# TensorE's instructions untied: placed by their emission order, and free to pass one another

## The chip, the cores and the metric

The kernel runs on one core of a Trainium2 chip. The core has a matrix engine (TensorE, PE in the profile, with PEld for the loading of its weights), VectorE (DVE), ScalarE (ACT), GpSimd (POOL), and SyncE (SP), whose queue issues most of the DMA transfers. Each engine takes its own instructions strictly in the order in which they stand in its queue; between engines, semaphores say when a result is there. Matmuls and transposes write to PSUM, which is cut into banks of 2 KB for each of 128 partitions; the other engines read the banks and so free them.

The metric is the device time of one execution in microseconds; less is better.

## What is computed

Two attentions follow one another. The first has 8 batches of 8 heads, 576 positions and 64 channels a head. Scores below the row's maximum less `tau` are dropped:

```python
scores = scale * np.matmul(q, k.transpose(0, 1, 3, 2))
thresh = np.max(scores, axis=-1, keepdims=True) - tau
scores = np.where(scores >= thresh, scores, -1000000000.0)
attn = softmax(scores)
attn_out = np.matmul(attn, v)
```

Its output, with the heads side by side as x of 576 rows by 512 columns for each batch, goes into a mixture of 4 attention experts of which each row takes its best two:

```python
logits = x @ w_gate                      # 4 a row; the two highest are kept
w = softmax(logits of the two)
for e in range(4):
    q, k, v = x @ wq[e], x @ wk[e], x @ wv[e]          # 64 channels
    a = softmax(causal(scale * (q @ k.T)))
    ye = a @ v @ wo[e]                                  # 512 columns
    out += (w of e, or 0 where e is not among the two) * ye
```

## The kernel before

**Units of work.** The first attention runs over 32 pairs of heads (n = 0 to 31, four to a batch). Each pair has five row tiles: four of 128 rows for each of the two heads, and one, called tile 4, that holds the last 64 rows of both. The main loop (from line 740) goes through 32 x 5 steps; step i takes tile s of pair n in the order `TS = (4, 0, 1, 2, 3)`. The second attention of a batch starts when its four pairs are done, and is spread over the steps of the next batch's pairs.

**The first attention.** `prep` (line 243) scales q and k (qi, ki), transposes them on TensorE (qkT; qkTt for the last 64 rows), splits each into a rounded part and its rest (hl), copies the small pieces (qd) and then spreads hl over partitions with DMAs on SP's queue: eight for the keys (kt), four for the queries (qt). `scores` (line 313) makes a score tile s in PSUM; VectorE finds its maximum (nmx, line 336) and the threshold (thr, line 338), ScalarE the exponential (line 341), VectorE drops what is under the threshold and sums (line 343), and POOL divides (line 351); the result is pp. `transp` (line 361) transposes pp on TensorE (tm, and tt for the last 64 columns) into a PSUM bank, from which ScalarE or VectorE copies it (pt, ptt; line 144 is the copy whose engine the scheduler picks). `attnv` (line 394) multiplies it with v (av) and splits the result into x's rounded part and rest ("xh", "xl", line 426).

**The second attention.** `project` (line 432) makes q2 and k2 of a pair of experts (bank pj); `values` (line 468) makes v2 and the logits, and at its end the gate weights gw. `scores2` (line 527) makes a score tile (s2 in the emitted names, s in the profile's), its maximum (nm) and exponential (p2, line 562). `scale2` (line 566) multiplies p2 on POOL by the gate and the inverse of its sum (line 576): it can run only when the last values of the batch, and the gate after them, are done. `transp2` (line 578) transposes p2 (t2, t2t), `attnv2` (line 601) multiplies it with v2, and `output` (line 626) makes o with wo.

**PSUM.** Score tiles of the first attention, and tile 4 of the second, take one of two double banks (`ps_s`). Everything else that TensorE writes takes one of four banks (`ps_g`) in rotation: the fifth such tile needs what was in the first to be read.

**What sets the order.** The program emits instructions; a scheduler then builds each engine's queue from their dependencies and priorities. `pr(what)` (line 103) sets the priority of what is emitted next: the step, plus an offset in steps from the table `PR`, plus a running number, so that a smaller value comes sooner. TensorE is the exception: `queued` (line 151) ties each matmul and transpose to the one emitted before it, so its queue is the emitted order whatever the table says.

```python
    def pr(what):
        now[1] += 20
        tc.cur_priority = 20000000 + int((now[0] + PR.get(what, 0.0)) * 1000000) + now[1]
```

The emitted order is worked out by a plan. `pe[1]` adds up a modelled time of TensorE in ns. Each step emits its own work and then `fill`s with pieces of the second attention up to the step's `goal`: outputs and transposes that are due, tile-4 scores, and otherwise one more group of projections or values (`project_some`, line 657). A piece is due some modelled ns after what it needs: `AFTER_S2` from a score tile to its transposes, `AFTER_T2` from there to its product, and `AFTER_V = 4500` from a batch's last values to the first transposes that need the gate (line 671). At most three probability tiles p2 are open (`P2B`).

Of the kernel before, what the change touches and what calls it, by code (L numbers as in the profile page):

```python
# [9 lines left out]
F32 = mybir.dt.float32  # L10
# [18 lines left out]
AFTER_S2, AFTER_V, AFTER_T2, AFTER_AV2 = 7000, 4500, 1800, 2000  # L29
BETWEEN_S2 = 2000  # L30
# [4 lines left out]
E_QD = "P"  # L35
# [13 lines left out]
    "s": 0.767, "max": -0.509, "thr": -0.091, "exp": 0.327, "stt": -2.461, "sum": -1.419, "nrm": 0.098,  # L49
# [4 lines left out]
}  # L54
PPB = 4
# [4 lines left out]
E_PT = "XX"  # L60
# [4 lines left out]
def kernel(  # L65
# [177 lines left out]
    def prep(n):  # L243
# [34 lines left out]
        def spread(dst, src):  # L278
            pr("dm")
            nc.sync.dma_start(dst.bitcast(F32), src.bitcast(F32))  # L280
# [10 lines left out]
        copy(E_QD, hl[:, :, KO + S:], hl[:, :, KO:KO + ST].bitcast(F32))  # L291
        for j, sl in enumerate(heads):
            pr("qd")
            copy(E_QD, qd[sl, :, j * ST:(j + 1) * ST], hl[sl, :, SM:KO].bitcast(F32))
        for x in range(2):
            for j, sl in enumerate(heads):

                o = KO if j else KO + ST
                for rows in heads:
                    spread(kt[rows, j, x], hl[sl, x, o:o + S])  # L300
# [60 lines left out]
    def transp(n, s):  # L361
# [4 lines left out]
        for j in range(2 if s < R else 1):  # L366
# [7 lines left out]
            copy(E_PT[j], pt, g)  # L374
# [203 lines left out]
    def transp2(b, t, ep):  # L578
        p2 = P2[b, t, ep][0]
        nch = min(t + 1, R)  # L580
        pts = []
        for j in range(2 if t < R else 1):
            g = gbank(f"t2_{b}_{t}_{ep}_{j}")
            pr("t2")
            for c in range(nch):
                transpose(g[:, c * P:(c + 1) * P], p2[:, j * SM + c * P:j * SM + (c + 1) * P])
            pr("pt2")
            pt = one.tile([P, SM], F32, tag="pt", name=f"pt2_{b}_{t}_{ep}_{j}", bufs=PTB)
            copy(E_PT2, pt[:, :nch * P], g[:, :nch * P])
            pts.append(pt)  # L590
# [237 lines left out]
```

## Time and profile before

| | us |
|---|---|
| runs | 1059.22, 1061.42, 1070.57 |
| median | 1061.42 |
| the profiled execution | 1066.01 |
| its span in the profile | 1064.3 |
| TensorE's mean granted clock in it | 0.984 of full speed |

The page's rows are groups of instructions: line, engine, operation, output<-inputs, how many; then busy time, mean ns of one, and the idle time of that engine just before them with what ended it. These are the groups of the main loop that do not stand in the prediction:

```profile
L351 POOL TENSOR_SCALAR pp<-pp,ss 128x576 f32<-128x576 f32 x288 | 212.4, 748 | 409.7 <-DVE ss L357 310.0
L343 DVE SCALAR_TENSOR_TENSOR pp<-s,thr,pp 128x576 f32<-128x576 f32 x288 | 234.2, 815 | 67.6 <-ACT pp L341 60.0
L341 ACT ACTIVATE pp<-s,nmx 128x576 f32<-128x576 f32 x288 | 214.9, 746 | 113.6 <-DVE nmx L336 112.0
L336 DVE TENSOR_REDUCE nmx<-s 128x1 f32<-128x576 f32 x288 | 215.8, 751 | 32.1 <-PE s L162 31.5
L162 PE MATMUL s<-kt,qt 128*128 128x288 f32 x1024 | 195.4, 314 | 25.6 <-DVE pp L343 10.7
```

A score tile costs VectorE 751 and 815 ns, ScalarE 746 and POOL 748. In the timeline a row has its start, its duration, and in brackets the engine's idle time ahead of it with what ended it. In the table of windows a row has the stretch, its length, the busy time of PE, PEld, DVE, ACT and POOL with their instructions, the granted clock, the DMA share and GB/s. Times count from the start of the span.

### The profile page before, as it was taken

To read this page: it belongs to the slowest core of one execution; us is meant where nothing else is said; L and a number is where in the kernel's file an instruction comes from. 1 tells how busy PE (TensorE), PEld (TensorE's weight loads), DVE (VectorE), ACT (ScalarE), POOL (GpSimd) and SP (SyncE) were. 2 spreads that over 40 slices of the span, in tenths; PEclk is the share of its full clock that TensorE was granted. 3 is DMA by queue.
4 is the path that set the end of the run, shared out by engine and by line. 5 is a ranking of instruction groups with operands and counts; after the bars stand their busy time and mean duration, and the time that the engine had idled before them with its cause. 6 is when DMAs were issued, how large, how long until landed. Compare 5 with 4: busy or idle time off the path is not lost.

```text
span 1064.3 us, 26639 instructions
## 1 busy us (share of the span) xinstructions
PE 966.1 (91%) x9520; PEld 860.6 (81%) x9520; DVE 833.5 (78%) x2411; ACT 636.6 (60%) x1556; POOL 407.8 (38%) x703
## 2 busy tenths in 40 slices
PE   3778979899899998999988999899989999899987
PEld 2777978789888898788887898778978789878875
DVE  3898886887878887888878888878787888778463
ACT  3676656665656665665656656666565756566553
POOL 2565433443434324353244433434343433433122
PEclk9999999999999999999999999999999999999998
DMA  6565421344322433324234442234432243320101
GB/s 164 140 162 143 118 78 33 97 125 108 99 68 56 122 98 99 99 72 116 68 87 99 110 121 70 53 87 124 120 98 58 55 132 99 76 55 13 46 2 45
DMA packets 83890, 96.11 MB, mean 90 GB/s; under 512 B 29744, under 2 KB 54320, under 8 KB 83760
## 3 DMA queue, kind: packets, MB, share of 16 engines
q1 hardware_dynamic: 83760, 94.42, 34.2%
q8 instruction: 76, 1.25, 0.5%
q14 instruction: 54, 0.44, 0.1%
HBM read 30.42 MB, written 9.44 MB: 37 GB/s over the span
## 4 chain that ended last, share of the span: by engine, by line
PE 60%; DVE 16%; ACT 11%; POOL 3%; issue 3%; DMA 0%; DVEq 0%; POOLq 0%; ACTq 0%
PE av L162 18%; PE s L162 13%; PE pj L162 8%; PE o L162 6%; PE tm L165 6%; DVE pp L343 5%; PE v L162 4%; PE t L165 3%; ACT p L562 3%; DVE x L426 2%; ACT pp L341 2%; ACT x L140 2%; POOL p L576 2%; DVE nmx L336 2%; ACT pt L144 2%
## 5 line engine op out<-in xcount | busy, mean ns | idle before, releaser
L351 POOL TENSOR_SCALAR pp<-pp,ss 128x576 f32<-128x576 f32 x288 | 212.4, 748 | 409.7 <-DVE ss L357 310.0
L343 DVE SCALAR_TENSOR_TENSOR pp<-s,thr,pp 128x576 f32<-128x576 f32 x288 | 234.2, 815 | 67.6 <-ACT pp L341 60.0
L341 ACT ACTIVATE pp<-s,nmx 128x576 f32<-128x576 f32 x288 | 214.9, 746 | 113.6 <-DVE nmx L336 112.0
L336 DVE TENSOR_REDUCE nmx<-s 128x1 f32<-128x576 f32 x288 | 215.8, 751 | 32.1 <-PE s L162 31.5
L162 PE MATMUL s<-kt,qt 128*128 128x288 f32 x1024 | 195.4, 314 | 25.6 <-DVE pp L343 10.7
L162 PEld LDWEIGHTS s<-kt,qt 128*128 128x128 f32 x1024 | 151.6, 194 | 38.0 <-issue 16.2
L165 PE MATMUL tm<-ident,pp 128*128 128x128 f32 x1152 | 162.4, 277 | 2.4 <-POOL pp L351 1.8
L162 PE MATMUL av<-pt,vm 128*64 128x128 f32 (+1 forms) x2560 | 157.2, 265 | 0.3
L144 ACT COPY pt<-tm 128x512 f32<-128x512 f32 x195 | 113.0, 588 | 61.7 <-PE tm L165 59.0
L165 PEld LDWEIGHTS tm<-ident,pp 128*128 128x128 f32 x1152 | 138.2, 143 | 4.2 <-POOL pp L351 3.7
L162 PEld LDWEIGHTS av<-pt,vm 128*64 128x64 f32 x2560 | 131.6, 137 | 11.9 <-issue 6.8
L562 ACT ACTIVATE p<-s,nm 128x384 f32<-128x384 f32 (+3 forms) x144 | 78.4, 549 | 66.5 <-DVE nm L560 64.5
L576 POOL TENSOR_SCALAR p<-p,sm,gw 128x512 f32<-128x512 f32 (+3 forms) x128 | 76.6, 606 | 82.6 <-ACT pt L144 33.9
L165 PE MATMUL t<-ident,p 128*128 128x128 f32 x384 | 65.0, 293 | 28.1 <-POOL p L576 21.3
L140 ACT ACTIVATE x<-av 128x256 fp32r<-128x256 f32 (+1 forms) x96 | 48.3, 503 | 70.4 <-PE av L162 49.0
L165 PEld LDWEIGHTS t<-ident,p 128*128 128x128 f32 x384 | 45.1, 147 | 41.5 <-POOL p L576 25.0
L560 DVE TENSOR_REDUCE nm<-s 128x1 f32<-128x384 f32 (+3 forms) x144 | 69.4, 512 | 9.4 <-PE s L162 5.9
L140 ACT ACTIVATE pt<-t 128x512 f32<-128x512 f32 (+2 forms) x144 | 58.7, 457 | 25.3 <-PE t L165 25.0
L144 DVE COPY pt<-tm 128x512 f32<-128x512 f32 x93 | 63.4, 684 | 6.6 <-PE tm L165 6.6
L162 PE MATMUL v<-wvh,x 128*128 128x260 f32 x320 | 67.0, 292 | 1.2 <-ACT p L562 0.3
L426 DVE TENSOR_TENSOR x<-av,x 128x256 fp32r<-128x256 f32 (+1 forms) x96 | 47.5, 494 | 23.1 <-ACT x L140 22.7
L162 PE MATMUL av<-ptt,vtz 128*64 128x128 f32 (+1 forms) x640 | 60.1, 263 | 0.0
(129 smaller groups left out, 1789.2 us busy)
## 6 DMA issues: line engine op xcount, KB each, us to landing
kt<-hl SPq DMA_DIRECT2D x256, 144.0 KB, 2.7
qt<-hl SPq DMA_DIRECT2D x128, 128.0 KB, 2.3
km<-in_k_dram SPq DMA_DIRECT2D x32, 256.0 KB, 2.9
qm<-in_q_dram SPq DMA_DIRECT2D x32, 256.0 KB, 3.0
vm<-in_v_dram SPq DMA_DIRECT2D x32, 256.0 KB, 2.8
out_dram<-ob SPq DMA_DIRECT2D x32, 256.0 KB, 2.4
km<-in_k_dram SPq DMA_DIRECT2D x32, 32.0 KB, 2.5
qm<-in_q_dram SPq DMA_DIRECT2D x32, 32.0 KB, 2.7
```

The source lines that it names most:

```text
L140: nc.scalar.activation(dst, src, AF.Copy)
L144: nc.any.tensor_copy(dst, src)
L162: queued(nc.tensor.matmul(out, x, y, **kw), x, ns if x.shape[0] == P else ns / 2)
L165: queued(nc.tensor.transpose(out, x, ident), x, 109)
L336: nc.vector.tensor_reduce(nmx[:, js], sv, axis=AX.XY, op=ALU.max, negate=True)
L341: nc.scalar.activation(e, sv, AF.Exp, bias=nmx[:, js])
L343: nc.vector.scalar_tensor_tensor(e, sv, thr[:, js], e, op0=ALU.is_ge, op1=ALU.mult, accum_out=ss[:, js])
L351: nc.gpsimd.tensor_scalar(p, p, ss[:, h:h + 1], 0.0, op0=ALU.mult, op1=ALU.add)
L426: nc.vector.tensor_tensor(xl, gs, xh.bitcast(F32), op=ALU.subtract)
L560: nc.vector.tensor_reduce(nmx[:, j:j + 1], sv, axis=AX.X if t < R else AX.XY, op=ALU.max, negate=True)
L562: nc.scalar.activation(p2[:, j * SM:j * SM + w] if t < R else halves(p2[:, :S]), sv, AF.Exp, bias=nmx[:, j:j + 1], accum_out=sm[:, j:j + 1])
L576: nc.gpsimd.tensor_scalar(p, p, sm[:, j:j + 1], gg[:, j:j + 1], op0=ALU.mult, op1=ALU.mult)
```

## The change

TensorE's instructions lose the tie: `queued` keeps only the modelled time. Their priority is the step and the running number alone (`TENSOR`, offset 0), so that the scheduler puts them in emitted order where they are ready in its own simulation, and otherwise lets a ready one pass. The table keeps the other engines' offsets, but that of "xl" goes from 0.858 to -0.15.

With it go changes of the plan and of the first pairs:

- `AFTER_V` is 8500 (5000 after the main loop, `AFTER_V_END`), and steps 0 and 2 call `project_some` once more, ahead of their own transposes. In step 2 `prep` goes on after the first `fill` and no longer before it. Tile 4 of the second attention's scores is emitted at a step's end and not by `piece`; `tiled` loses its argument.
- The loads of pairs 1 and 2 stand in SP's queue behind the last spread of pair 0 (`SPREAD[0]`). For pair 0, the key spreads of its second head go to ScalarE's queue (behind `SPREAD[1]`, the last split), qd is copied by VectorE, and tau is loaded first, on ScalarE's queue.
- Copies of tm out of PSUM go to ScalarE for pairs 0 to 3; from pair 4 on the scheduler picks ScalarE or VectorE as before (`E_PT` goes).
- `transp2` puts both experts' transposes in one bank with one copy where they fit (tiles 0 and 1).

```diff
-AFTER_S2, AFTER_V, AFTER_T2, AFTER_AV2 = 7000, 4500, 1800, 2000
-BETWEEN_S2 = 2000
+AFTER_S2, AFTER_V, AFTER_T2, AFTER_AV2 = 7000, 8500, 1800, 2000
+BETWEEN_S2, AFTER_V_END = 2000, 5000
...
-    "av": -4, "xh": -0.154, "xl": 0.858, "pj": 1.006, "q2": -0.353, "v2": 0.393, "v2e": 0.385,
+    "xh": -0.154, "xl": -0.15, "q2": -0.353, "v2e": 0.385,
...
+TENSOR = ("s", "qkT", "tm", "tt", "av", "pj", "v2", "s2", "t2", "av2", "o")
-E_PT = "XX"
...
-        tc.cur_priority = 20000000 + int((now[0] + PR.get(what, 0.0)) * 1000000) + now[1]
+        tc.cur_priority = 20000000 + int((now[0] + (0.0 if what in TENSOR else PR[what])) * 1000000) + now[1]
...
     def queued(r, x, ns):
-        if pe[0] is not None:
-            tc.add_manual_dep(r.ins, pe[0].name,
-                              mybir.DependencyInfo(mybir.DependencyClass.NoSync, mybir.DependencyReason.DATA),
-                              reason="order")
...
+        def load(dst, src):
+            r = nc.sync.dma_start(dst, src)
+            if n in (1, 2):
+                tc.add_manual_dep(r.ins, SPREAD[0].name, NOSYNC, reason="order")
...
-        def spread(dst, src):
+        def spread(dst, src, e=nc.sync):
             pr("dm")
-            nc.sync.dma_start(dst.bitcast(F32), src.bitcast(F32))
+            r = e.dma_start(dst.bitcast(F32), src.bitcast(F32))
+            if n == 0 and e is nc.sync:
+                SPREAD[0] = r.ins
+            elif n == 0:
+                tc.add_manual_dep(r.ins, SPREAD[1].name, NOSYNC, reason="order")
...
-        copy(E_QD, hl[:, :, KO + S:], hl[:, :, KO:KO + ST].bitcast(F32))
+        e = "D" if n == 0 else E_QD
+        copy(e, hl[:, :, KO + S:], hl[:, :, KO:KO + ST].bitcast(F32))
...
+        spread_keys(0)
+        if n:
+            spread_keys(1)
         yield
         main(qi, 0)
...
+        if not n:
+            spread_keys(1, nc.scalar)
...
-            copy(E_PT[j], pt, g)
+            copy("A" if n < NPAIR else "X", pt, g)
...
-        for j in range(2 if t < R else 1):
-            g = gbank(f"t2_{b}_{t}_{ep}_{j}")
+        for js in ([list(range(nj))] if nj * nch <= R else [[j] for j in range(nj)]):
+            g = gbank(f"t2_{b}_{t}_{ep}_{js[0]}")
...
-                    T2[len(T2) - len(unscaled):] = [(pe[1] + AFTER_V, *x) for x in unscaled]
+                    T2[len(T2) - len(unscaled):] = [(pe[1] + (AFTER_V if now[0] < N else AFTER_V_END), *x) for x in unscaled]
...
-        elif S2 and S2[0][2] == R and len(T2) < P2B:
-            score_tile()
...
+    tau_t = const.tile([P, 1], F32, name="tau_t")
+    pr("ld")
+    nc.scalar.dma_start(tau_t, bass.AP(tensor=tau.tensor, offset=tau.offset, ap=[[0, P], [1, 1]]))
     load_pair(0)
...
+        if s in (0, 2):
+            project_some()
         next(tr, None)
...
-        next(pre, None)
+        if s != 2:
+            next(pre, None)
         fill(goal - 0.6 * share)
+        if s == 2:
+            next(pre, None)
...
         fill(goal)
+        if S2 and S2[0][2] == R and len(T2) < P2B:
+            score_tile()
```

The names in the rows that follow carry the batch or pair, then the tile, the half or head and a running number; "x4" stands for as many of the same kind in a row.

TensorE's queue before, around the first transposes of batch 3's second attention (t2_3_4 transposes tile 4; pj_3 are batch 3's projections, s_17 and tm_17 pair 17 of the first attention):

```order
L162 MATMUL pj_3_1_0_1_0_8054<-x0_3_3_7223,wqh_106 128x288
L162 MATMUL pj_3_1_0_1_0_8054<-x1_3_3_7224,wqh_106 128x288
L162 MATMUL pj_3_1_0_1_0_8054<-x0_3_3_7223,wql_107 128x288
L162 MATMUL s_17_2_1_8027<-kt_17_7295,qt_17_7294 128x288 x4
L165 MATMUL tm_17_0_1_8083<-ident_73,pp_17_0_7786 128x128 x4
L165 MATMUL tt_17_0_8090<-ident_73,pp_17_0_7786 128x128
L165 MATMUL t2_3_4_0_0_8094<-ident_73,p2_3_4_0_7618 128x128 x4
```

And the same place now:

```order
L159 MATMUL pj_3_1_1_1_0_8074<-x0_3_3_7195,wkl_109 128x288
L159 MATMUL s_17_3_0_8093<-kt_17_7282,qt_17_7281 128x288 x4
L162 MATMUL tm_17_1_0_8103<-ident_73,pp_17_1_7871 128x128 x4
L162 MATMUL tm_17_1_1_8110<-ident_73,pp_17_1_7871 128x128 x4
L162 MATMUL tt_17_1_8117<-ident_73,pp_17_1_7871 128x128
L162 MATMUL t2_3_4_0_0_8121<-ident_73,p2_3_4_0_7612 128x128 x4
```

The transposes t2_3_4 came after the second of the four pj groups of experts 2 and 3 (pj_3_1_0_1) and tile 0's transposes of pair 17; now they come after the fourth (pj_3_1_1_1), one more score tile and tile 1's transposes.

TensorE's queue before, ahead of the small transpose qkTt_15 of pair 15's preparation (s2_2 and t2_2 belong to batch 2's second attention; s_14, tm_14 and tt_14 to pair 14):

```order
L162 MATMUL s2_2_0_0_1_6450<-mask_80,ident_b_78 128x128
L162 MATMUL s_14_1_0_6472<-kt_14_5826,qt_14_5825 128x288 x4
L165 MATMUL tm_14_4_0_6482<-ident_73,pp_14_4_6335 128x128 x4
L165 MATMUL tt_14_4_6489<-ident_73,pp_14_4_6335 128x128
L165 MATMUL qkTt_15_6494<-ident_73,qi_118 128x128
```

And now:

```order
L162 MATMUL t2_2_2_0_1_6465<-ident_73,p2_2_2_0_5932 128x128 x3
L159 MATMUL s2_2_4_1_6473<-q2_2_1_1_6104,q2d1_122 128x288 x6
L159 LDWEIGHTS ident_b_78
L159 MATMUL s2_2_4_1_6473<-mask2_85,ident_b_78 128x64
L159 MATMUL s_14_1_0_6491<-kt_14_5832,qt_14_5831 128x288 x4
L162 MATMUL tm_14_4_0_6501<-ident_73,pp_14_4_6326 128x128 x4
L162 MATMUL tt_14_4_6508<-ident_73,pp_14_4_6326 128x128
L162 MATMUL t2_2_1_0_0_6513<-ident_73,p2_2_1_0_6306 128x128 x4
L162 MATMUL qkTt_15_6520<-ident_73,qi_118 128x128
```

The bank that qkTt_15 takes was that of a score tile (s2_2_0_0_1) whose last write stood ten matmuls ahead; it is now that of transposes (t2_2_2_0_1), and a tile-4 score group of seven matmuls and four transposes stand between as well.

SP's DMA queue before, from the sixth transfer on (the first five load pair 0: km, qm, vm_0; kt_0 and qt_0 are pair 0's spreads):

```order
L730 DMA tau_t_132<-in_tau_dram 128x1
L189 DMA vm_1_177<-in_v_dram 128x2x256
L189 DMA vm_2_431<-in_v_dram 128x2x256
L187 DMA km_97<-in_k_dram 128x2x256
L188 DMA km_97<-in_k_dram 64x2x64
L187 DMA qm_96<-in_q_dram 128x2x256
L188 DMA qm_96<-in_q_dram 64x2x64
L191 DMA vtz0_100<-in_v_dram 64x64 x2
L191 DMA vtz1_101<-in_v_dram 64x64 x2
L280 DMA kt_0_140<-hl_0_138 64x576 x8
L280 DMA qt_0_139<-hl_0_138 64x512 x4
```

And now, from the fifth:

```order
L184 DMA vm_0_126<-in_v_dram 128x2x256
L184 DMA vtz0_100<-in_v_dram 64x64 x2
L282 DMA kt_0_140<-hl_0_138 64x576 x4
L282 DMA qt_0_139<-hl_0_138 64x512 x4
L184 DMA km_97<-in_k_dram 128x2x256
L184 DMA km_97<-in_k_dram 64x2x64
L184 DMA qm_96<-in_q_dram 128x2x256
L184 DMA qm_96<-in_q_dram 64x2x64
L184 DMA vm_1_177<-in_v_dram 128x2x256
```

The loads of pairs 1 and 2 stood ahead of pair 0's spreads and now stand behind them; four of the eight key spreads, and tau, are on ScalarE's queue.

More of the change, by code (lines that the diff above doesn't have):

```diff
@@ L48 @@
 PR = {
-    "s": 0.767, "max": -0.509, "thr": -0.091, "exp": 0.327, "stt": -2.461, "sum": -1.419, "nrm": 0.098,
[4 rows of a table removed]
+    "max": -0.509, "thr": -0.091, "exp": 0.327, "stt": -2.461, "sum": -1.419, "nrm": 0.098,
[4 rows of a table added]
 }
+TENSOR = ("s", "qkT", "tm", "tt", "av", "pj", "v2", "s2", "t2", "av2", "o")
 PPB = 4
@@ L231 @@
     QK = {}
+    SPREAD = [None, None]
     def zeros(name, n=2):
@@ L276, in main, with spread_keys @@
             split(slice(o, o + SM), g)
-        def spread(dst, src):
+        def spread(dst, src, e=nc.sync):
             pr("dm")
-            nc.sync.dma_start(dst.bitcast(F32), src.bitcast(F32))
+            r = e.dma_start(dst.bitcast(F32), src.bitcast(F32))
[3 more added lines that the diff above has]
+                tc.add_manual_dep(r.ins, SPREAD[1].name, NOSYNC, reason="order")
+        def spread_keys(j, e=nc.sync):
+            o = KO if j else KO + ST
+            for x in range(2):
+                for rows in heads:
+                    spread(kt[rows, j, x], hl[heads[j], x, o:o + S], e)
         main(ki, KO + ST)
@@ L290, in prep @@
         pr("qd")
-        copy(E_QD, hl[:, :, KO + S:], hl[:, :, KO:KO + ST].bitcast(F32))
+        e = "D" if n == 0 else E_QD
+        copy(e, hl[:, :, KO + S:], hl[:, :, KO:KO + ST].bitcast(F32))
         for j, sl in enumerate(heads):
             pr("qd")
[L294 to L300, printed above, removed]
+            copy(e, qd[sl, :, j * ST:(j + 1) * ST], hl[sl, :, SM:KO].bitcast(F32))
+        spread_keys(0)
+        if n:
+            spread_keys(1)
         yield
@@ L580, in transp2 @@
         nch = min(t + 1, R)
+        nj = 2 if t < R else 1
         pts = []
-        for j in range(2 if t < R else 1):
-            g = gbank(f"t2_{b}_{t}_{ep}_{j}")
+        for js in ([list(range(nj))] if nj * nch <= R else [[j] for j in range(nj)]):
+            g = gbank(f"t2_{b}_{t}_{ep}_{js[0]}")
             pr("t2")
-            for c in range(nch):
-                transpose(g[:, c * P:(c + 1) * P], p2[:, j * SM + c * P:j * SM + (c + 1) * P])
+            for j in js:
+                for c in range(nch):
+                    o = (j - js[0]) * nch + c
+                    transpose(g[:, o * P:(o + 1) * P], p2[:, j * SM + c * P:j * SM + (c + 1) * P])
             pr("pt2")
-            pt = one.tile([P, SM], F32, tag="pt", name=f"pt2_{b}_{t}_{ep}_{j}", bufs=PTB)
-            copy(E_PT2, pt[:, :nch * P], g[:, :nch * P])
-            pts.append(pt)
+            pt = one.tile([P, SM], F32, tag="pt", name=f"pt2_{b}_{t}_{ep}_{js[0]}", bufs=PTB)
+            w = len(js) * nch * P
+            copy(E_PT2, pt[:, :w], g[:, :w])
+            pts += [pt[:, (j - js[0]) * nch * P:] for j in js]
         if t == R:
@@ L716, in fill, with tiled @@
             pass
-    def tiled(most=1):
+    def tiled():
         for _ in range(2):
@@ L722, in tiled @@
                 value_tile()
-        for _ in range(most):
-            if S2 and S2[0][2] < R and len(T2) < P2B:
-                score_tile()
+        if S2 and S2[0][2] < R and len(T2) < P2B:
+            score_tile()
     now[0] = -10
+    tau_t = const.tile([P, 1], F32, name="tau_t")
+    pr("ld")
+    nc.scalar.dma_start(tau_t, bass.AP(tensor=tau.tensor, offset=tau.offset, ap=[[0, P], [1, 1]]))
     load_pair(0)
-    tau_t = const.tile([P, 1], F32, name="tau_t")
-    nc.sync.dma_start(tau_t, bass.AP(tensor=tau.tensor, offset=tau.offset, ap=[[0, P], [1, 1]]))
     tau_p = const.tile([P, 1], F32, name="tau_p")
```

12 lines of the change are left out of this document (7 added, 5 removed), and 6 rows, old and new, of the table PR.

## Prediction, made before the changed kernel ran

> **What bounds the kernel now.** The page's first line and the chain of waits come first. They name TensorE: nine tenths busy, six tenths of the chain that ended last, and on its chain no one line above a fifth.
> ```profile
> PE 966.1 (91%) x9520; PEld 860.6 (81%) x9520; DVE 833.5 (78%) x2411; ACT 636.6 (60%) x1556; POOL 407.8 (38%) x703
> PE 60%; DVE 16%; ACT 11%; POOL 3%; issue 3%; DMA 0%; DVEq 0%; POOLq 0%; ACTq 0%
> ```
> The change removes no matmul, so what it can win is the time in which TensorE stands still. The table of windows cuts the span into start, the first four pairs, the steady stretch and the end (us, busy per engine, granted clock).
> ```profile
> 1.00:53.00 52.00, 30.00 (x238) 25.93 (x238) 31.41 (x89) 24.72 (x47) 23.06 (x61) 0.97 0.60 155
> 53.00:106.00 53.00, 43.00 (x474) 39.51 (x473) 46.36 (x132) 36.61 (x77) 32.46 (x60) 0.97 0.62 152
> 106.00:960.00 854.00, 799.09 (x7939) 716.08 (x7940) 693.43 (x2003) 520.70 (x1278) 324.16 (x534) 0.99 0.35 91
> 960.00:1064.00 104.00, 94.01 (x875) 79.03 (x873) 62.19 (x190) 54.55 (x156) 27.72 (x45) 0.97 0.07 24
> ```
> TensorE idles 22 us in the start, 10 in the next stretch (there VectorE is the fuller engine, 46.4 of 53), 55 in the steady one, 10 at the end. The list of waits for TensorE between 106 and 960 us (sum, times, longest) says what ended them.
> ```profile
> PE t L165 <- POOL p L576: 18.7, 7, 3.8
> PE qkTt L165 <- ACT p L562: 8.7, 13, 0.8
> PE s L162 <- DVE pp L343: 4.8, 22, 0.5
> PE t L165 <- ACT pt L140: 4.3, 6, 0.7
> PE t2t L165 <- ACT pt L140: 3.8, 5, 0.8
> PE tt L165 <- ACT p L562: 3.4, 7, 0.5
> PE t L165 <- ACT pt L144: 1.9, 6, 0.6
> PE tt L165 <- ACT pt L144: 1.8, 6, 0.3
> PE o L162 <- ACT pt L144: 1.1, 6, 0.2
> ```
> One wait of 2.5 to 3.8 us falls once in each batch; the rest are short waits for a PSUM bank that ScalarE has yet to empty.
>
> **1. The wait behind the values, once a batch.** The first transposes of the second attention need its probabilities scaled by the gate, and the gate needs the last values. In batch 3:
> ```profile
> 534.13 0.43 PE L162 MATMUL pj<-x,wqh 128*128 128x288 f32 x2
> 537.06 0.52 PE L162 MATMUL pj<-x,wqh 128*128 128x288 f32 x2
> 538.73 0.70 PE L162 MATMUL s<-kt,qt 128*128 128x288 f32 x4
> 539.27 0.60 PE L165 MATMUL tm<-ident,pp 128*128 128x128 f32 x4
> 539.70 0.27 PE L165 MATMUL tt<-ident,pp 128*128 128x128 f32 x1
> 542.64 1.11 PE L165 MATMUL t<-ident,p 128*128 128x128 f32 x4 [2.67 <-POOL p L576]
> 542.60:546.00 3.40, 3.36 (x17) 3.36 (x18) 0.72 (x5) 1.49 (x3) 3.10 (x6) 0.55 0.34 96
> ```
> The last value matmul ends where that pj starts, at 534.1; the scaled tile is ready at 542.6, 8.5 us later, and TensorE has work for 5.8 of them. AFTER_V goes from 4500 to 8500, and project_some() is called once more in steps 0 and 2, so that in TensorE's order t2_3_4_0_0 moves back. Where two groups of pj stood between the last values and t2, four stand now (pj_3_1_0_0 to pj_3_1_1_1) and three score tiles instead of two. By the starts of these rows (twelve pj 537.06 to 538.73, 1.67 us; four s 0.54; four transposes 0.43) that is about 12 us of work against 8.5 needed. The stall goes, with 3.5 us to spare; the POOL and gate work keeps its time beside it. So -18.7.
> The clock goes with it: behind that idle stretch 3.4 us ran at 0.55, which costs 3.4 x 0.45 = 1.5 us, seven times 10.7. Sum of the step -29.4 (from -18.7, if the clock falls anyway, to -31).
> [...]
>
> **2. The transpose qkTt, 31 times.** It takes the PSUM bank that the score tile four allocations earlier left, and which the exponential (line 562) must read:
> ```profile
> 434.74 0.78 PE L162 MATMUL s<-kt,qt 128*128 128x288 f32 x4
> 436.61 0.33 PE L165 MATMUL qkTt<-ident,qi 128*128 128x128 f32 x1 [0.55 <-ACT p L562]
> ```
> qkTt's bank is now that of t2_2_2_0_1, which a copy empties. Between the bank's last write and qkTt_15 lay the score group, five transposes and a mask, 1.1 us; now there are a second score group of six and four transposes more, 2.4 us. Over all pairs no distance is under 1.5 but that of pair 0. The wait was 0.5 to 0.8 at 1.1, so -8 of 8.7 (0 to -8.7).
>
> **3. The other bank waits** are the rows t, t2t, tt and o of the list: 4.3 + 3.8 + 3.4 + 1.9 + 1.8 + 1.1 = 16.3. What empties a bank, by engine:
> ```profile
> L144 DVE COPY pt<-tm 128x512 f32<-128x512 f32 x93 | 63.4, 684 | 6.6 <-PE tm L165 6.6
> L144 ACT COPY pt<-tm 128x512 f32<-128x512 f32 x195 | 113.0, 588 | 61.7 <-PE tm L165 59.0 <-PE qkTt L165 0.9
> ```
> A bank is safe when some 0.9 us of TensorE work lie between its last write and its next use: ScalarE's copy of 0.59 and the two signals. Summing over one batch what each use lacks of 0.9 gives 5.0 us in the order before and 2.3 now (uses under 0.6 us apart: ten, then one). So 16.3 x 0.55 = -9 (0 to -16).
>
> **4. The start.** SP's queue, and what TensorE waited for there:
> ```profile
> 11.83 5.03 SPq L280 DMA_DIRECT2D kt<-hl  x8
> 16.96 2.47 SPq L280 DMA_DIRECT2D qt<-hl  x4
> qt<-hl SPq DMA_DIRECT2D x128, 128.0 KB, 2.3
> PE s L162 <- DMA qt<-hl: 5.1, 1, 5.1
> PE s L162 <- POOL qd L133: 3.4, 1, 3.4
> PE s L162 <- DVE thr L338: 4.8, 3, 2.4
> PE s L162 <- DVE pp L343: 5.1, 3, 2.8
> ```
> (The last two rows are those of 53 to 106 us.) Ahead of the first qt stand eight spreads of 0.63 us and the loads of pairs 1 and 2. Now four spreads go to ScalarE's queue, the loads stand behind the first qt, qd is copied by VectorE, and tau is first on ScalarE's queue.
> ```profile
> 7.29 0.83 ACT L258 ACTIVATE qi<-qm,qsc 128x640 f32<-128x640 f32 x1 [1.24 <-DVE qsc L734]
> 9.24 0.28 DVE L267 TENSOR_TENSOR hl<-qkTt,hl 128x128 fp32r<-128x128 f32 x1
> 19.98 1.30 PE L162 MATMUL s<-kt,qt 128*128 128x288 f32 x4 [5.05 <-DMA qt<-hl]
> ```
> tau earlier takes the 1.24 away: the last part of hl ends at 9.5 - 1.2 = 8.3, three copies of about 0.3 on VectorE at 9.2, and SP, long idle by then, starts the spreads. Four of them and the first two of qt are issued by 13, 2.3 more makes 15.3 against 20.0: -4.7. ScalarE holds four issues of about 0.63, between 9 and 12, when the first scores are not yet there. Pair 1's keys are issued later, at some 14, and land in about the same 2.3 to 3; their transpose, which follows the first two score groups, can come at 18: just covered. I take -4.5 (0 to -6).
>
> **5. Who empties what.** The two rows above are the evictions pt<-tm. In the order now VectorE has 53 of them, so it loses 40 x 0.684 = 27 us and ScalarE gains 40 x 0.588 = 23.5; joining the small transposes takes 32 copies from ScalarE. ScalarE is 60% busy, so this is hidden in the steady stretch; were it not, it would show as waits of one copy, 0.6. It pays in pairs 0 to 3, where VectorE's 8 copies (5.5 us) fall away and 9.9 us of TensorE's waits hang on VectorE: -3 (0 to -5.5). The earlier remainder of x ("xl") and the moved last score tile cost nothing: same instructions, VectorE has room.
>
> **6. What it costs.** Free order breaks groups apart. Counted over the whole order, TensorE changes between full matmuls, half-width (av) and half-height (s of the second attention) 266 times before and 328 now. Price:
> ```profile
> 548.67 0.69 PE L162 MATMUL s<-kt,qt 128*128 128x288 f32 x4
> 549.29 0.69 PE L162 MATMUL av<-pt,vm 128*64 128x64 f32 x16
> ```
> Four s take 0.54 us before a transpose (538.73 to 539.27, above) and 0.62 before av, so about 0.1 a change: 62 x 0.1 = +6 (+5 to +12).
> [...]
> New waits, since VectorE keeps 81% of a shorter steady stretch and seven transposes now stand 0.4 us behind one that VectorE empties: +4 (0 to +20).
>
> **Sum:** -29.4 - 8 - 9 - 4.5 - 3 + 6 + 4 = -43.9. The profiled execution took 1066.0 (span 1064.3): 1022. The median shown is 4.6 lower, which would give 1017.5. I say 1020.
>
> **Rivals.**
> VectorE takes over. For: 81% in the steady stretch, and 22 waits of s for line 343. Against: they are 0.5 at most, and it loses 22 us there. Then steps 2 and 3 come back as such waits and 1, 4 and 6 stay: 1066 - 29.4 - 4.5 + 6 = 1038, median 1034 to 1050.
> The clock falls anyway. The stretch at 0.55 is made of transposes too; if they count for less as work than matmuls, moving the wait away leaves it. Then 10.7 less, 1033, median about 1030. Against it: the transposes at 539.27 run as fast as 0.44 us for four. [...]
> Matmuls passed forward block what they passed. In the order now the 64 av groups of the first attention fall into 91 pieces, mostly around a score group; TensorE takes its queue in order, so if PSUM is not free on the chip, the rest of av waits. In pairs 0 to 3 such waits average (5.1 + 4.8) / 6 = 1.65; over 27 cuts that is 45 us and cancels the gain, at 2.8 it is 76 and the result 1094. Against: the distance to the freeing instruction is under 3.5 us four times a batch before and twice now. It decides from 1.6 us a cut, and is slower by 1% from 2.0.
> The wait only moves: t2 is later, and the three buffers of the second attention's probabilities hold its score tiles back as long. Against: the projections that fill the gap are work of the same batch. Gain under 10 us: 1051 to 1066.
>
> **Chances** (1% is about what a measurement tells from no change): forecast, 1000 to 1034, 0.60; VectorE 0.16; clock 0.04; the wait only moves 0.08; blocked 0.07; better than 1000, 0.05. Faster 0.60 + 0.16 + 0.04 + 0.05 = 0.85, same 0.08, slower 0.07. The range 1000 to 1051 leaves out the last three, 0.20.
>
> **What would show it.** On the chain the same row of two batches lies 127.4 us apart:
> ```profile
> 540.27 2.32 POOL p L576 x3
> 667.66 2.32 POOL p L576 x3
> ```
> Right: no wait of t for POOL p over 1 us between 106 and 960 and no 0.55 window; qkTt gone from the list; first s on kt at 15 to 16 us; that period near 121; VectorE's pt copies near 53. Wrong: waits of s for line 343 above 20 us in the steady stretch, or gaps inside av groups.

## The result and the profile after

The changed kernel takes 1033.09 us (median of four, 1032.28 to 1036.05), the kernel before 1061.61 (median of four); the ratio is 0.972, with a 95% interval of 0.966 to 0.978. The forecast was 1020, with a range of 1000 to 1051. The profiled execution took 1033.4 (span 1031.7), where the sum gave 1022.

The page's first line, and its chain by engine, for the changed kernel:

```profile
PE 966.5 (94%) x9520; PEld 863.5 (84%) x9520; DVE 816.5 (79%) x2374; ACT 651.6 (63%) x1564; POOL 408.4 (40%) x700
PE 59%; DVE 17%; ACT 13%; issue 5%; POOL 4%; DMA 1%; SPq 0%; DVEq 0%; ACTq 0%; POOLq 0%
```

TensorE's busy time is what it was (966.1); the span lost 32.6 us of its idle time. To see where, both kernels are cut at the same work: the first matmul of the tile-4 scores (s<-hl,qd) of pair 0, of pair 4 and of pair 31. So there is the start, then pairs 0 to 3, in which the second attention has nothing to do yet, then the middle, then the end. The table of windows cut there, of before:

```profile
13.10:105.80 92.70, 70.17 (x698) 63.42 (x698) 75.33 (x210) 57.07 (x117) 49.72 (x96) 0.96 0.61 151
105.80:966.10 860.30, 804.60 (x8018) 720.61 (x8016) 699.30 (x2021) 525.39 (x1289) 328.60 (x540) 0.99 0.35 90
966.10:1064.30 98.20, 88.70 (x798) 74.68 (x798) 56.49 (x174) 49.91 (x145) 23.28 (x39) 0.97 0.07 25
```

and of the changed kernel:

```profile
10.40:110.60 100.20, 78.23 (x698) 68.67 (x698) 72.51 (x203) 60.19 (x122) 50.32 (x95) 0.91 0.61 153
110.60:938.60 828.00, 800.06 (x8043) 719.88 (x8043) 685.26 (x1993) 538.60 (x1302) 332.03 (x545) 1.00 0.36 94
938.60:1031.70 93.10, 85.88 (x772) 72.95 (x771) 56.40 (x168) 48.70 (x134) 22.11 (x37) 0.98 0.08 27
```

| us | before | forecast change | after | change |
|---|---|---|---|---|
| start and pairs 0 to 3 | 105.8 | -4.5 - 3 = -7.5 | 110.6 | +4.8 |
| middle | 860.3 | -29.4 - 8 - 9 + 6 + 4 = -36.4 | 828.0 | -32.3 |
| end | 98.2 | 0 | 93.1 | -5.1 |
| sum | 1064.3 | -43.9 | 1031.7 | -32.6 |

So the middle came close to its sum, the start and the first four pairs went the other way, and the end won what no step had forecast. The list of waits for TensorE in the middle of the changed kernel (sum, times, longest) is whole here:

```profile
PE t L162 <- DVE ss L369: 8.9, 7, 1.3
PE pj L159 <- ACT ptt L140: 4.0, 7, 0.6
PE tm L162 <- ACT p L575: 2.8, 7, 0.4
PE t L162 <- DVE x L439: 2.6, 7, 0.6
PE tm L162 <- POOL p L589: 2.3, 7, 0.3
PE s L159 <- DVE zl L642: 1.8, 7, 0.3
PE av L159 <- ACT p L575: 1.2, 7, 0.2
PE tm L162 <- POOL pp L364: 0.5, 1, 0.5
```

24.1 us; the same list of before, whose main rows stand in the prediction, adds up to 51.6. The wait for the gate (18.7), those of qkTt (8.7) and those of s for line 343 (4.8) are gone. In their place stands a wait of 1.3 us at the same transposes, now for VectorE. The timeline shows what that is:

```profile
531.87 1.04 PE L162 MATMUL tm<-ident,pp 128*128 128x128 f32 x8
532.74 0.32 PE L162 MATMUL tt<-ident,pp 128*128 128x128 f32 x1
532.76 0.82 POOL L589 TENSOR_SCALAR p<-p,sm,gt 128x576 f32<-128x576 f32 x1
533.01 0.82 DVE L356 SCALAR_TENSOR_TENSOR pp<-s,thr,pp 128x576 f32<-128x576 f32 x1 [0.22 <-ACT pp L354]
533.75 0.45 DVE L474 TENSOR_TENSOR q<-pj,q 128x288 fp32r<-128x288 f32 x1
534.35 0.63 PE L162 MATMUL t<-ident,p 128*128 128x128 f32 x4 [1.28 <-DVE ss L369]
```

TensorE arrives at 533.06. The scaled tile is there at 533.58, half a microsecond later; the rest is a PSUM bank. These transposes take the bank of the last pj group, four tiles back in the emitted order, and VectorE subtracts from it (line 474) only behind a score row, until 534.20. The name that the list gives, ss, is a VectorE row that ended a little later (534.28).

### The profile page after: what moved, and what is told of

Same layout as the page of the kernel before. It is cut to its first block, busy times and chain, and to the rows that moved or that the text cites. A ratio compares the mean times of both kernels' runs of the same rounds, so it can differ in the third digit from the quotient of the medians.

```text
span 1031.7 us, 26572 instructions
## 1 busy us (share of the span) xinstructions
PE 966.5 (94%) x9520; PEld 863.5 (84%) x9520; DVE 816.5 (79%) x2374; ACT 651.6 (63%) x1564; POOL 408.4 (40%) x700
## 4 chain that ended last, share of the span: by engine, by line
PE 59%; DVE 17%; ACT 13%; issue 5%; POOL 4%; DMA 1%; SPq 0%; DVEq 0%; ACTq 0%; POOLq 0%
PE av L159 18%; PE s L159 13%; PE tm L162 8%; PE pj L159 7%; DVE pp L356 5%; PE v L159 4%; PE o L159 4%; ACT p L575 3%; ACT pp L354 3%; PE t L162 3%; DVE nmx L349 3%; DVE x L439 2%; ACT pt L144 2%; PE qkT L162 2%; POOL pp L364 2%
## 5 line engine op out<-in xcount | busy, mean ns | idle before, releaser
L159 PE MATMUL s<-kt,qt 128*128 128x288 f32 x1024 | 205.3, 319 | 5.8 <-DMA qt<-hl 5.4
L162 PE MATMUL tm<-ident,pp 128*128 128x128 f32 x1152 | 166.2, 278 | 22.1 <-POOL pp L364 15.8
L159 PE MATMUL av<-pt,vm 128*64 128x128 f32 (+1 forms) x2560 | 167.8, 267 | 0.0
L162 PEld LDWEIGHTS tm<-ident,pp 128*128 128x128 f32 x1152 | 136.1, 143 | 33.2 <-POOL pp L364 22.6
L159 PEld LDWEIGHTS av<-pt,vm 128*64 128x64 f32 x2560 | 140.0, 138 | 15.4 <-issue 11.4
L573 DVE TENSOR_REDUCE nm<-s 128x1 f32<-128x384 f32 (+3 forms) x144 | 71.1, 513 | 24.2 <-PE s L159 21.4
L162 PE MATMUL t<-ident,p 128*128 128x128 f32 x384 | 61.1, 284 | 15.9 <-DVE ss L369 8.9
L159 PE MATMUL av<-ptt,vtz 128*64 128x128 f32 (+1 forms) x640 | 68.8, 263 | 0.0
L159 PE MATMUL v<-wvh,x 128*128 128x260 f32 x320 | 64.8, 287 | 0.0
L162 PEld LDWEIGHTS t<-ident,p 128*128 128x128 f32 x384 | 43.0, 144 | 25.9 <-POOL p L589 14.3
L159 PE MATMUL av<-pt,v 128*64 128x128 f32 (+1 forms) x896 | 57.9, 262 | 1.9 <-ACT p L575 1.2
```

What stands on the lines that cost most here:

```text
L159: queued(nc.tensor.matmul(out, x, y, **kw), x, ns if x.shape[0] == P else ns / 2)
L162: queued(nc.tensor.transpose(out, x, ident), x, 109)
L573: nc.vector.tensor_reduce(nmx[:, j:j + 1], sv, axis=AX.X if t < R else AX.XY, op=ALU.max, negate=True)
```

## The experiments

All times of the stages, by the same cuts, of every kernel that ran ("run": median, or the one time; the kernel before had medians of 1065 to 1068 beside these runs; a kernel without a ratio ran once, and the stages are those of one profile each):

| kernel | start + pairs 0 to 3 | middle | end | run | ratio to before |
|---|---|---|---|---|---|
| before | 13.1 + 92.7 | 860.3 | 98.2 | 1061.61 | |
| changed | 10.4 + 100.2 | 828.0 | 93.1 | 1033.09 | 0.972 |
| changed, tied throughout (e1) | 10.2 + 98.5 | 829.6 | 98.3 | 1035.76 | 0.969 |
| changed, tied in pairs 0 to 3 (e3) | 10.4 + 96.0 | 827.1 | 93.4 | 1028.67 | 0.964 |
| before, untied (e2) | 14.0 + 99.8 | 821.3 | 97.8 | 1035.14 | 0.968 |
| changed, AFTER_V 4500 (e5) | 10.2 + 100.0 | 810.7 | 136.4 | 1059.39 | |
| start of the change, plan of before, tied in pairs 0 to 3 (e10) | 10.1 + 97.4 | 822.2 | 95.1 | 1026.54 | 0.962 |
| changed, av tied (e7) | 10.1 + 97.5 | 823.3 | 92.7 | 1024.74 | 0.959 |
| changed, copies to either engine (e4) | 10.1 + 103.1 | 826.8 | 95.7 | 1037.36 | |
| changed, keys on SyncE (e8) | 10.4 + 100.4 | 827.8 | 93.9 | 1034.25 | |
| e10 with av tied (e11) | 10.4 + 98.6 | 832.8 | 95.1 | 1035.41 | 0.971 |
| before, untied but for pairs 0 to 3 and av (e12) | 13.8 + 95.6 | 824.4 | 95.2 | 1029.57 | 0.967 |
| before, AFTER_V 8500 (e6) | 13.4 + 95.8 | 832.6 | 98.5 | 1041.97 | |
| before, with the start of the change (e13) | 10.2 + 96.0 | 858.1 | 96.9 | 1062.99 | |

**The plan or the freed order?** One kernel takes the freedom back, one takes it alone, one takes it back in pairs 0 to 3, and one takes back the due time.

e1, the changed kernel:

```diff
     def queued(r, x, ns):
+        if pe[0] is not None:
+            tc.add_manual_dep(r.ins, pe[0].name, NOSYNC, reason="order")
```

> The changed kernel with TensorE's instructions tied again in emitted order; everything else of the change stays. Stages are cut at the first matmul of the tile-4 scores (s<-hl,qd) of pairs 0, 4 and 31: up to pair 0 (13.1 us before, 10.4 changed), pairs 0 to 3 (92.7 before, 100.2 changed), pairs 4 to 30 (860.3, 828.0), and the rest (98.2, 93.1). Theory 1: the plan (later due time, more projections) brings the gain of the middle stage, and the freed order is what loses 7.5 us in pairs 0 to 3, by letting the transposes tm pass score tiles and then wait for POOL. Then pairs 0 to 3 take 88 to 93 us with no wait of tm for POOL pp over 1 us, the middle 822 to 832, the run 1015 to 1026. Rival A: the loss in pairs 0 to 3 is the copies of tm that all go to ScalarE there: they still take 99 to 101, the run 1028 to 1035. Rival B: the middle's gain comes from passing: the middle takes over 845 with the bank waits back, the run over 1042.

e2, the kernel before, without those lines and with the offsets of the names in TENSOR at 0.

> The kernel before with only the tie removed and TensorE's offsets set to 0 (due times, start, copies as before). Theory 1: pairs 0 to 3 take 97 to 102 us instead of 92.7, the middle 855 to 868 with the wait for the gate still there (2.7 us a batch), the run 1063 to 1078. Rival B (passing brings the gain): the middle takes 830 to 845, the run 1030 to 1050. Rival A: pairs 0 to 3 stay at 92 to 94.

Theory 1 fell in both: in e1 the middle came as expected, but pairs 0 to 3 took 98.5 and not 88 to 93; in e2 the middle should have kept the wait for the gate. The change without the freed order (e1) gives 829.6 in the middle, the freed order alone (e2) gives 821.3, and the two together give 828.0, more than e2. e1 has no wait of t for POOL p left in the middle; e2 has one, of 2.9 us, in its first batch (before: seven). How the freed order does it stands on VectorE. First and last VectorE rows of the gate in batch 3, with the large rows between them; before:

```profile
535.19 0.24 DVE L500 TENSOR_TENSOR cmp<-lg 128x80 f32<-128x80 f32 x1
...
536.40 0.45 DVE L461 TENSOR_TENSOR q<-pj,q 128x288 fp32r<-128x288 f32 x1
...
537.07 0.75 DVE L336 TENSOR_REDUCE nmx<-s 128x1 f32<-128x576 f32 x1
...
538.69 0.65 DVE L267 TENSOR_TENSOR hl<-qkT,hl 128x512 fp32r<-128x512 f32 x1
539.26 0.81 DVE L343 SCALAR_TENSOR_TENSOR pp<-s,thr,pp 128x576 f32<-128x576 f32 x1
...
540.09 0.75 DVE L336 TENSOR_REDUCE nmx<-s 128x1 f32<-128x576 f32 x1
540.87 0.42 DVE L520 COPY gt<-gw 64x2 f32<-64x2 f32 x2
```

and with only the tie removed (e2):

```profile
525.57 0.24 DVE L497 TENSOR_TENSOR cmp<-lg 128x80 f32<-128x80 f32 x1 [0.42 <-ACT lg L141]
...
527.28 0.45 DVE L458 TENSOR_TENSOR q<-pj,q 128x288 fp32r<-128x288 f32 x1
...
527.79 0.74 DVE L333 TENSOR_REDUCE nmx<-s 128x1 f32<-128x576 f32 x1
...
529.09 0.34 DVE L517 COPY gt<-gw 64x2 f32<-64x2 f32 x2
529.47 0.69 DVE L264 TENSOR_TENSOR hl<-qkT,hl 128x512 fp32r<-128x512 f32 x1
```

Three large rows (hl, pp, nmx) stand no longer inside the gate's work but behind it. TensorE's queue holds the same two pj groups and two score tiles between the last values and the transposes as before; but from the start of the last value matmul to the scaled tile it takes 6.0 us and no longer 8.4 to 8.6 (in the first batch 8.2 and 9.1). That the scheduler moved VectorE's rows because its own times for TensorE had changed is likely, but not shown. In the changed kernel the same stretch takes 13.4 us: the last values come where VectorE has more of other work, and the additional TensorE work covers most of it. It takes 13.4 us in e1 too, which is tied, and 6.0 in e10 below, which has the plan of before: the plan lengthens it.

e3 restores the tie only `if now[0] < 4 * (R + 1)`.

> The changed kernel with TensorE's instructions tied in the first 20 steps only (pairs 0 to 3). Theory 1 (the freed order loses in pairs 0 to 3 alone): these take 88 to 93 us and the middle stays at 827 to 829, the run 1021 to 1026. Rival A (the copies on ScalarE): pairs 0 to 3 take 99 to 101, the run 1032 to 1035. Against the run that is tied throughout, the difference is what passing is worth in the middle and at the end: minus 6 if the 50 or so broken av groups cost 0.1 us a change of shape and nothing else depends on it, plus 10 or more if passing avoids bank waits.

The tie in pairs 0 to 3 gives 4.2 us there and 4.4 in the median; less than expected (88 to 93 us there, 1021 to 1026 for the run), the middle as expected. Against e1, passing in the middle is worth 2.5 us (829.6 to 827.1): the list of waits falls from 35.1 to 23.8 us, and TensorE's busy time, with the broken groups, rises from 791.5 to 799.9.

e5 puts 4500 back for AFTER_V.

> The changed kernel with AFTER_V at 4500 again; the additional projections of steps 0 and 2 stay. TensorE's queue then holds 7.6 us of work between the last values and the first transposes of a batch, where it holds 11.7, and before it held 5.7. Theory 1: the scaled probabilities come some 10.9 us after the last values, so a wait of t for POOL p of about 2.5 us a batch is back in place of the 1.3 for DVE, with a stretch of lower clock behind it: the middle 843 to 855, the run 1048 to 1060. Rival C: the additional projections, and not the due time, took the wait away: the middle stays at 826 to 834.

The run is in its range, but its stages don't answer: a part of the second attention's work slid behind the main loop (7605 matmuls in the middle instead of 8043, and 136.4 us at the end). The wait of t for POOL p is back (6.9 us, 6 times), behind another of 2.0 us for VectorE (thr) that was not expected. By the batch's period (125.5 to 126.5 us from the third batch to the last, against 122.4) the due time is worth 3 to 4 us a batch, much of it clock: the middle of e5 has a granted clock of 0.98, which over 810.7 us is about 16 us by estimate, where the changed kernel's middle lost none. The clean trial of it is e6, the kernel before with that one number changed:

```diff
-AFTER_S2, AFTER_V, AFTER_T2, AFTER_AV2 = 7000, 4500, 1800, 2000
+AFTER_S2, AFTER_V, AFTER_T2, AFTER_AV2 = 7000, 8500, 1800, 2000
```

> The kernel before, tied, with AFTER_V 8500 alone. TensorE's queue then holds 8.8 us between the last values and the first transposes instead of 5.7, and VectorE's rows among the gate's are those of before, so the scaled probabilities still come 8.4 to 8.9 us after the last values. By the prediction's first term the wait of t for POOL p (18.7 us) falls to 0 to 4 and the stretches at 0.55 go: the middle takes 830 to 836 us instead of 860.3, the other waits for banks as before. Rival: the clock's share is not won, since a shorter wait of another kind keeps it low: 838 to 845. Rival: the wait only moves to score tiles, as the prediction's last rival has it: over 850.

As expected: 832.6. The table of windows has the clock at 1.00 there:

```profile
109.20:941.80 832.60, 796.01 (x8018) 711.34 (x8016) 691.24 (x2013) 528.06 (x1296) 330.30 (x540) 1.00 0.36 93
```

The list of waits in the middle begins so, and has no row of t for POOL p; the waits for banks are as before:

```profile
PE qkTt L165 <- ACT p L562: 8.6, 13, 0.8
PE s L162 <- DVE pp L343: 4.9, 22, 0.9
```

One number alone thus wins 27.7 us in the middle, where the whole change wins 32.3 (one profile each).

**Do plan and freedom add?** e10 is the changed kernel, tied in the first 20 steps, with the plan of before (4500, no additional `project_some`, `prep` and tile 4's scores where they were).

> The changed kernel with its instructions tied in the first 20 steps only, and with the plan of before in the middle: AFTER_V 4500, no additional projections, prep ahead of the first fill, tile 4's scores by piece. Start, copies, joined transposes and xl stay as changed. Theory 2: the wait for the gate went away by two ways that replace each other. Freed order lets the scheduler put fewer other VectorE rows between those of the gate (last values to gt copies 4.5 us with only the tie removed, 6.8 before, 11.2 changed); the plan puts more TensorE work ahead of the transposes. Together the gate is later and the transposes wait 1.3 us for a bank that VectorE empties. Then without the plan the gt copies come 4.4 to 4.8 us after the last values, the middle takes 819 to 824, pairs 0 to 3 take 92 to 97, the run 1015 to 1027. Rival: the plan has a part of its own in the middle (fewer short bank waits): the middle stays at 827 to 832, the run 1026 to 1033.

822.2, and from the second batch on the gt copies are done 4.5 to 4.7 us after the last values: they replace each other, as expected. In the first batch the copies take 6.9 us and a wait of 2.9 us for the gate stays. Pairs 0 to 3 missed their range by 0.4.

**What do the broken av groups cost?** e7 ties each av matmul of the first attention to what is emitted ahead of it (`if at_av[0]`, set around the loops of `attnv`).

> The changed kernel with the first attention's av matmuls tied to what is emitted ahead of them, all else free: changes of shape on TensorE 276 instead of 328. If a change costs 0.1 us, as the prediction took, the middle takes 822 to 825 (about 46 of the 52 fall there); by the busy time of the kernel tied throughout (791.5 us in the middle against 800.1, with 58 changes fewer) it would be 0.15, and the middle 820 to 822. Rival: av passing ahead fills waits: the middle takes 829 to 836. Pairs 0 to 3 stay at 98 to 101, since there the transposes tm still pass score tiles.

The middle falls by 4.7 us, 0.11 us for each of the 42 changes of shape that went there (257 to 215 by the trace). Pairs 0 to 3 fell too, by 2.7, which was not expected: the transposes tm still pass score tiles there, and TensorE still waits for POOL as often (13.8 us, 8 times, against 15.3). Ten changes of shape went there (26 to 16), which at 0.11 is 1.1 of the 2.7, and the shorter waits are 1.5. So the cut av groups are the larger part of the 4.2 us that e3 won with all tied, and the passing of tm, which theory 1 blamed, is at most the rest. This kernel is the fastest that ran, 0.959 of before (0.956 to 0.962).

e11 does the same to e10, and e12 is the kernel before with only the tie removed from step 20 on, but for av.

> The mixed kernel (tied in the first 20 steps, plan of before in the middle, the change's start, copies and joined transposes) with the first attention's av matmuls tied to what is emitted ahead of them: changes of shape 274 instead of 312. If whole av groups save 0.1 us a change and this adds to the shorter gate chain, the middle takes 817 to 820 us (822.2 without), start and pairs 0 to 3 together 105 to 109, the end 92 to 96, the run 1016 to 1025, the fastest of all. Rival: both draw on the same slack, and the middle stays at 821 to 824.

> The kernel before, with only this changed: the tie is removed from step 20 on, except for the av matmuls of the first attention; offsets of TensorE's instructions 0. Start, copies, due time, plan and transposes are those of before. By the theory that freed order alone shortens the gate chain: gt copies 4.4 to 4.8 us after the last values, the middle 816 to 821, start and pairs 0 to 3 together 104 to 108 (105.8 before), the run 1017 to 1026. Against the mixed kernel with whole av groups, the difference is what start, copies and joined transposes are worth: the prediction had 4.5 + 3 for the first two; if the gain of the start is lost again by pair 4, it is 0 to 4.

Both missed. With the plan of before, whole av groups cost: the middle is 832.8 (822.2 in e10) and 824.4 (821.3 in e2). TensorE's busy time falls in e12 (794.9 us against 799.1 in e2), but score tiles now wait for VectorE behind the unbroken groups, 9.4 us (20 times) in e11 and 8.4 in e12, where e10 and e2 had 0.4. In e11 the clock falls as well (below): 6.8 of its 10.6 us are the clock's, by losses in the middle of 10.2 us against 3.4 in e10. So passing ahead fills waits where the plan is that of before; with the longer due time whole groups bring such waits of 1.3 us only (e7). The gain that e12's text looked for in start, copies and joined transposes did not show: e11 has all three and is 5.8 us slower than e12.

**Copies and start.** e4 gives the copies of tm to either engine in pairs 0 to 3:

```diff
-            copy("A" if n < NPAIR else "X", pt, g)
+            copy("X", pt, g)
```

> The changed kernel with the copies of tm in pairs 0 to 3 given to either engine again, as before. TensorE's order in these pairs stays. Rival A (the copies on ScalarE lose there): pairs 0 to 3 take 92 to 96 us, and 19 or so of their copies are VectorE's. Theory 1 (order and the clock that falls in longer waits): 99 to 102, with the 3 us waits of tm for POOL pp as they are. The prediction had these copies as a gain of 3 us, so by it 103.

103.1, with six of these copies on VectorE (eight before, none in the changed kernel): rival A falls, and the 2.9 us agree with the prediction's 3. It is one run, and the order of TensorE's rows differs a little from 85 us on.

e8 issues the second head's keys behind the queries on SyncE's queue.

> The changed kernel with the second head's four key spreads of pair 0 on SyncE's queue, behind the queries, instead of on ScalarE's queue. In the changed kernel qt lands 3.9 us after its issue (median of four) where it took 2.3 before, and the first score tile on kt comes at 17.6 us. Theory: the eight spreads of two queues share the DMA engines, which are full from 10 to 18 us. Then qt lands in 2.3 to 2.8 us and the first score tile comes at 15.8 to 16.6; the second head's tile, 20 to 21. Rival: issue on SyncE sets it: the first tile stays at 17.2 to 17.8.

The DMA table between 8 and 30 us, from issue to landing, of before, of the changed kernel and of e8 (one row each):

```profile
qt<-hl SPq DMA_DIRECT2D x4, 128.0 KB, 2.3
```

```profile
qt<-hl SPq DMA_DIRECT2D x4, 128.0 KB, 3.9
```

```profile
qt<-hl SPq DMA_DIRECT2D x4, 128.0 KB, 2.7
```

With two queues at once the queries landed later, after 3.9 us, against 2.3 before and 2.7 in e8, where SyncE's queue has all the spreads; the DMA share from 14.4 to 18.4 us is 1.06 in the changed kernel and 0.89 in e8. That the two queues' transfers held one another up is likely, but not shown. In e8 the first score tile on kt comes at 16.1 us instead of 17.6, as expected, and the second at 18.7, earlier than expected; but start and pairs 0 to 3 together take 110.8 us against 110.6, so nothing is won in sum.

e13 is the kernel before with the start of the change alone.

> The kernel before, tied, with the change's start alone (tau first on ScalarE's queue, the second head's key spreads of pair 0 on ScalarE's queue, loads of pairs 1 and 2 behind the spreads, qd on VectorE). Theory: pair 0 comes 2.5 to 3 us earlier (first score on kt at 17.4 to 17.8 us), but pairs 1 to 3 are set by VectorE, ScalarE and POOL and by their own later loads, so that start and pairs 0 to 3 together take 104 to 108 us (105.8 before). The prediction: 101.3, 4.5 less. The middle stays at 857 to 863.

As expected, the first score on kt comes at 17.4 and start and pairs 0 to 3 take 106.2. Pair 0's tile 4 comes 2.9 us earlier, and by pair 1 the lead is 0.2: TensorE then waits 1.5 us for pair 1's keys, which POOL scales (ki), and whose load now stands behind the spreads. What is left by pair 4 can't be said: before, e6 and e12 have the same rows in the same order on every engine up to there and took 105.8, 109.2 and 109.5; e13, with 106.2, lies between them.

## Why the prediction was right, and where it was not

The forecast was a gain of 41 us in the run, and 28.5 came. The mechanism that carried it, the wait for the gate in the middle, was right. Of the 11.3 us by which the profiled sum missed, 12.3 are the start and pairs 0 to 3 and 4.1 the middle, and the end, which no step had, gave 5.1 back by luck. The number alone would have said little: 1033 stands beside the 1030 of the rival on the clock and just below the 1034 from which the one on VectorE begins.

**Step 1, the wait for the gate.** The removal was right: the wait of t for POOL p was 18.7 us and is gone from the list, and e6 wins 27.7 by the due time alone. The clock's share came out by luck. Its loss in the middle, added up in windows of 2 us, was 10.2 us before and is 0.0 now, and the prediction had 10.7 for a fall behind each of the seven waits. But the trace of before has a fall behind only four of them (at 160, 416, 542 and 925 us) and none behind the other three. Two windows of before, behind the waits of 2.45 us that end at 287.4 and at 414.9 (the clock is the third number from the end):

```profile
287.80:289.80 2.00, 2.00 (x20) 2.00 (x18) 0.83 (x4) 1.63 (x3) 1.81 (x5) 1.00 0.60 148
415.80:417.80 2.00, 2.00 (x12) 1.99 (x11) 0.52 (x3) 1.58 (x3) 1.81 (x5) 0.53 0.41 131
```

The other two falls, at 310 and 819 us, stand behind short waits for banks, those of steps 2 and 3:

```profile
307.80 0.33 PE L165 MATMUL qkTt<-ident,qi 128*128 128x128 f32 x1 [0.62 <-ACT p L562]
310.25 0.69 PE L165 MATMUL t<-ident,p 128*128 128x128 f32 x2 [0.71 <-ACT pt L140]
309.80:311.80 2.00, 1.55 (x7) 1.47 (x8) 1.07 (x3) 1.60 (x6) 0.45 (x2) 0.58 0.51 137
```

So 6.8 us of clock were lost behind the gate's waits, in four falls of 1.7, and 3.4 behind bank waits. e6 lost none of the 10.2, though its bank waits stayed; why those two falls went with the due time is open.

Wrong was "the POOL and gate work keeps its time beside it": the scaled tile came 13.4 us after the last values, not 8.5, because VectorE has more of other rows among the gate's. The 3.5 us to spare were used up, and 0.5 us of each 1.3 is still a wait for POOL. The step also took the due time for the one cause; e2 shows that the freed order alone does it by another way, in six batches of seven.

**Steps 2 and 3, the banks.** qkTt went to nothing, as forecast (-8.7); it is gone in e1 too and stays at 5.6 us in e2 and 5.7 in e10, so the plan removed it. The other bank waits and the new ones were put at -9 and +4. The list had 24.2 us before beside the gate and qkTt, and has 24.1 now: the old ones went, with those of s for line 343, and eight new kinds came. The largest, 8.9 us at the seven transposes behind a bank that VectorE empties, is the one that the prediction named. The new waits are the term that was sized too small: of the 24.1 us now, 20 were forecast in all.

**Step 4, the start.** -4.5 was forecast. The first score on kt came 2.4 earlier, at 17.6 and not at 15.3. The step that failed is the landing taken as 2.3 us, which is 3.9 beside ScalarE's queue; the spreads also started at 10.0 and not at 9.2, and "just covered" for pair 1's keys was 1.5 short in e13.

**Step 5, the copies.** e4 agrees, with 2.9, and VectorE has 53 of them, as counted.

**Step 6, what free order costs.** Right in the middle: 4.7 by e7, 0.11 us a change. Not seen was that a price is paid in pairs 0 to 3 too, 2.7 us, by the changes and by longer waits for POOL.

**Pairs 0 to 3.** By the sum, start and pairs 0 to 3 together were to take 98.3 us, and the changed kernel took 110.6. Its copies won 2.9, about as forecast, and the cut av groups lost 2.7. The rest is partly luck: the profile of before, on which the sum stood, was a lucky one in this stage. e6 and e12, with the same rows up to there, took 3.4 and 3.7 us more. In e6 four matmuls of s take 1.27 to 1.31 us until 34.7 us, where before has 0.77 at 23.9. The windows show a clock of 1.00 for the slow rows at the start, so the losses added up from windows leave them out; these are 3.4 us before, 6.8 in e6 and 8.5 in the changed kernel. Against e6 and e12 the change lost about 1 us up to pair 4, where it should have won 7.5; how much of the start's 4.5 is left there, e13 doesn't tell. That free order itself brings the longer waits behind which the clock falls is suggested by the other free kernels (99.8 to 103.1 but for e7), not shown; e1, which is tied, took 98.5. Here TensorE idles most, and the timeline of pair 2 shows the form that the wait has now:

```profile
70.52 0.78 PE L159 MATMUL s<-kt,qt 128*128 128x288 f32 x4
74.36 0.66 PE L162 MATMUL tm<-ident,pp 128*128 128x128 f32 x4 [3.06 <-POOL pp L364]
74.85 0.60 PE L162 MATMUL qkT<-ident,qi 128*128 128x128 f32 x4
75.32 0.94 PE L159 MATMUL s<-kt,qt 128*128 128x288 f32 x4
```

Before, the score tile stood ahead of tm and waited 2.39 us for VectorE at the same place.

**The end** won 5.1 us that no step had. e1, which has the change's transposes and its due time, keeps 98.3, but with a clock's loss of 6.8 us against 1.8 in the changed kernel, so the clock alone accounts for the difference between these two. Against before (3.4) it accounts for 1.6 of the 5.1; the rest is open.

**The rivals.** VectorE did not take over: no wait of s for line 343 (now 356) is left in the middle. The clock did not fall anyway: the middle lost nothing to it. The wait didn't merely move: 51.6 us became 24.1. "Matmuls passed forward block what they passed" shows in pairs 0 to 3 alone, where tm waits 15.3 us for POOL; before, score tiles waited 14.8 there for VectorE (8.4 and 6.4) and tm 1.8 for POOL.

## What to carry to other kernels

Where a wait can be removed by putting work ahead of it or by making what it waits for earlier, try each alone: here either gave 28 to 39 us in the middle, and both together less than the better one. A scheduler that is told less on one engine also rearranges the others, so read their queues as well before costing a change of order. And let ready work pass, but keep groups whole whose matmuls have another shape than those around them (0.11 us a change in e7), if nothing waits behind them; that is a matter of trial, since the same tie won 4.7 us under one plan and lost 3 to 11 under another, the clock's falls included.

## What the runs showed of the hardware

The clock fell in pieces of one size. The losses of stages, added up from windows, are 1.7, 3.4, 6.8, 8.5 and 10.2 us: about multiples of 1.7. In the kernel before, each of the six falls of the middle is a stretch of 3.4 us at 0.50, by windows of 0.4 us. And in e11 one came without a long wait. TensorE's rows around 441 us of e11 with their idle time ahead, and the windows behind them (the clock is the third number from the end):

```profile
441.37 0.33 PE L165 MATMUL tt<-ident,pp 128*128 128x128 f32 x1 [0.51 <-ACT pt L144]
442.78 0.78 PE L162 MATMUL s<-kt,qt 128*128 128x288 f32 x4 [1.08 <-DVE pp L359]
```

```profile
442.00:444.00 2.00, 1.22 (x14) 1.06 (x16) 2.00 (x8) 1.46 (x4) 0.75 (x2) 0.87 0.01 4
444.00:446.00 2.00, 2.00 (x30) 2.00 (x28) 1.52 (x6) 0.74 (x1) 2.00 (x4) 0.50 0.03 8
```

A fall followed 0.51 and 1.08 us of idle time within 2 us there, while none followed 1.28 us in one piece, in each batch of the changed kernel. From the second batch on the falls of e11 begin at 443.5, 689.2 and 935.0 us, two batches apart, with none in the batches between. Before, waits of the same 2.45 us were followed by a fall at 415 us and by none at 287. So the length of the wait alone does not decide; what else does, is not shown. Before, e6 and e12, whose rows are the same up to pair 4, took 105.8, 109.2 and 109.5 us to get there: a change of less than 4 us can't be read from one profile of before in that stage. The changed kernel and e5, equal up to there as well, took 110.6 and 110.2.
